# A decode-attention kernel: the first weight load issued ahead of the program's entry barrier

## The chip, the cores and the metric

The kernel runs on one core of one Trainium2 chip. The metric is the time of one execution in microseconds (us), as the device counts it; every time quoted is the median of several executions. The profile's span (first to last instruction) is 1.7 to 2.0 us shorter than that time, in every run. The ranges are quoted with the medians.

The engines are called TensorE (PE in the profile), VectorE (DVE), ScalarE (ACT), GpSimd (POOL) and SyncE (SP).

## The reference

One token passes through a layer norm; attention over a key and a value cache of 8 groups with 65,536 keys each runs beside a small dense block with GELU; both results are added to x.

```python
x = A_x                                       # 1 x 1 x 512, bf16
xn = layernorm(x)
q = xn @ wq                                   # 512 x 4096
s = q . k_cache * 128 ** -0.5                 # k_cache: 8 x 65536 x 128, four heads to a group
o = softmax(s) . v_cache                      # v_cache: 8 x 65536 x 128
out = x + o @ wo + (gelu(xn @ w1 + b1) @ w2 + b2)
```

The two caches are 134 MB each, wq and wo 4 MB each, w1 and w2 1.8 MB each: 280 MB have to be read once, and very little else is large.

## The kernel before

All bulk loads are issued by SyncE on one DMA queue, in the order in which they are used: wq, w1, w2, then K and V pieces of 4 or 8 MB as their buffers come free, then wo. The three small inputs (x, b2, b1) are issued by ScalarE on its own queue.

```python
def dma_small():                              # ScalarE's queue
    sch.dma(ACT, lambda: act.dma_start(out=rows_bf[0:1, :], in_=A_x[0]), sem_x, writes=["row0"])
    ...                                       # b2 and b1 likewise

def dma_wq():                                 # SyncE's queue
    sch.dma(SP, lambda: sp.dma_start(out=wq_sb, in_=A_wq.rearrange("(p kt) n -> p kt n", kt=KT)),
            csem[NK], writes=["va"])
...
dma_small()
dma_wq()
dma_w12()
issue_chunks()                                # K0 and K1; V0 only when the dense block has left its buffer
```

Operations are first recorded per engine (`SP.ops` and so on, each with its waits and the semaphore that it raises) and written out at the end, one block per engine. Ahead of these blocks stands what the framework puts at the head of every program: GpSimd writes four constants, then all five engines meet at a barrier. Each engine drains itself and raises one semaphore; GpSimd waits for four of these and releases the others. (In the trace of the kernel before, the four drains start between 0.00 and 0.32 us, GpSimd's last constant is finished at 0.45, its wait for the four starts at 0.54, and the others are released at 0.66 to 0.68.) No load needs the constants.

Then come the layer norm (VectorE, from x), the q projection (TensorE, from wq), the dense block (w1, w2), and 16 rounds over pairs of K pieces and a V piece. `va` and `vb` are the two halves of the V buffer. They hold wq, w1 and w2 first, so the first V load is issued only when the dense block is through.

Of the kernel before, what the change touches and what calls it, by code (L numbers as in the profile page):

```python
# [183 lines left out]
def _emit(eng_obj, ops):  # L184
    for waits, fn, pub in ops:
        for s, v in waits:
            eng_obj.wait_ge(s, v)
        if fn is None:
            continue
        ins = fn()  # L190
        if pub is not None:
            ins.then_inc(pub[0], pub[1])


def _emit_rolled(eng_obj, ops, marks, holder=None):
    folded, growth = _fold([ops[a:b] for a, b in zip(marks, marks[1:])])
    _emit(eng_obj, ops[:marks[0]])
    _emit_loop(eng_obj, folded, growth, len(marks) - 1, holder)
    _emit(eng_obj, ops[marks[-1]:])
# [38 lines left out]
def bass_parallel_sum__gqa_block_cached__dense_activation_gelu__decode_kernel(  # L238
# [48 lines left out]
    SP = sch.add_engine("sp", "sp")  # L287
# [49 lines left out]
    while g0 < GE:  # L337
        n = next(m for m in (4, 2, 1) if g0 + m <= GE)
# [487 lines left out]
    )  # L826
    sch.wait_ev(SP, ev_out)

    with nc.Block() as block:

        @block.gpsimd
        def _(e):
            _emit(e, POOL.ops)

        @block.sync
        def _(e):
            _emit(e, SP.ops)

        @block.scalar
        def _(e):  # L840
            _emit_rolled(e, ACT.ops, [m[1] for m in marks2])

        @block.vector
        def _(e):
            _emit_rolled(e, DVE.ops, [m[0] for m in marks2], pair)

        @block.tensor
        def _(e):
            _emit_rolled(e, PE.ops, marks)
# [28 lines left out]
```

## Time and profile before

| | before |
|---|---|
| time | 658.46 us (658.15 to 658.76, 3 runs) |
| span, TensorE busy, granted TensorE clock | 656.5 us, 82%, 0.767 |
| read from HBM | 280.50 MB, 427 GB/s over the span |
| wq issued, first wq packet, barrier open | 0.75, 1.79, 0.66 us |
| last weight piece landed | 653.7 us |

Lines of the page, kernel before: the span, the DMA engines' busy share in tenths and the rate in each of 40 slices, and the chain of work that ended last by engine.

```profile
span 656.5 us, 27968 instructions
...
DMA  8999999999999999999999999999999999999997
GB/s 369 438 436 426 429 430 433 439 425 461 401 441 439 421 453 413 437 427 445 433 417 449 417 445 421 427 457 411 447 419 447 429 419 441 423 459 408 431 433 295
...
DMA 63%; PE 34%; issue 2%; DVE 0%; SPq 0%
...
```

The DMA engines are busy at 90% or more in all slices but the first and the last, and 63% of the last chain is waiting for DMA. Between the 50th and the 200th MB the packets' records show (200 - 50) MB / (466.32 - 120.13) us = 433 GB/s. Whether the stream could run faster is not shown here; the change leaves its rate as it is and goes for time in which the stream doesn't run, before its first packet at 1.79 us.

The timeline of the kernel before, from 0 us; the columns are start, duration, engine (SPq and ACTq are the sequencers that issue loads), line, operation and tiles.

```profile
...
0.33 0.12 POOL L863 MEMSET const-uint8-127<- 128x1 uint8 x1
0.74 0.53 ACTq L454 DMA_DIRECT2D rows_bf<-in_A_x_dram  x1
...
0.75 0.39 SPq L463 DMA_DIRECT2D kv<-in_A_wq_dram  x1
...
1.20 0.41 SPq L467 DMA_DIRECT2D kv<-in_B_w_dram  x1
...
2.95 0.40 DVE L499 CAST x_row<-rows_bf 1x512 f32<-1x512 bf16 x1
...
8.75 0.16 DVE L521 CAST xnT_bf<-pA 128x4 bf16<-128x4 f32 x1 [0.38 <-PE pA L518]
...
13.13 3.53 PE L525 MATMUL pss<-kv,xnT_bf 128*1 128x512 bf16 x32 [4.42 <-DMA kv<-in_A_wq_dram]
...
```

GpSimd's last constant is finished at 0.45 us, the barrier opens, and SyncE issues wq at 0.75 us. x has landed before VectorE takes it up at 2.95 us; the layer norm's end (L521) is at 8.91 us; and TensorE's q projection (L525) waits, by the bracket, for wq, until 13.13 us.

The waits of SyncE's queue in the kernel before (waited for: us in total, times, longest):

```profile
...
SPq L434 <- PE pst L590: 350.8, 30, 17.1
...
SPq L863 <- PEq L863: 0.7, 1, 0.7
...
```

The second line is the entry barrier: SyncE stands there for 0.7 us. The first is the opposite: SyncE waits 30 times for TensorE to free a K buffer, 351 us in total, and this costs nothing, as enough loads are in the queue meanwhile. That can be counted. With the bytes of all loads issued, less the bytes of all packets finished, at each issue of SyncE, the least that was outstanding in the kernel before is 2.33 MB (at 113.90 us), which is 5.4 us of work at 433 GB/s. The queue is never empty between its first and its last packet. The packets' records agree: from 2.5 us to 640 us at least 13 packets are in flight at every moment, and nearly always 16 or more.

The end of the last chain in the kernel before, in order of time (start, duration, what):

```profile
...
585.82 28.78 DMA kv<-in_A_k_cache_dram
...
636.99 16.42 DMA kv<-in_A_wo_dram
653.41 0.14 issue
653.55 0.63 PE pss L805 x13
...
654.20 0.29 DVE fin_bf L820
```

### The profile page before, as it was taken

The page shows a single profiled execution, that of the slowest core. Times are in us where ns is not written, and L with a number is a line of the kernel's source. Part 1 is how long each engine was busy: PE and PEld are TensorE (multiplying, and loading weights), DVE is VectorE, ACT ScalarE, POOL GpSimd, SP SyncE. Part 2 cuts the span into 40 slices and gives each one's busy share as a digit, 9 for nine tenths or more (in the row PEclk, how much of TensorE's full clock was granted, in tenths as well). Part 3 has the DMA queues.
Part 4 walks back from the last instruction along what each step waited for, and adds up shares of the span by engine and source line. Part 5 has one row for each costly group of instructions (what it writes and reads, how often), then busy time and mean ns, then how long its engine had stood idle before and what let it go on. Part 6 is the DMA issues. An engine that isn't in the chain of part 4 may idle for free.

```text
span 656.5 us, 27968 instructions
## 1 busy us (share of the span) xinstructions
PE 539.3 (82%) x12682; PEld 512.1 (78%) x12682; DVE 275.7 (42%) x574; ACT 244.9 (37%) x454; POOL 2.9 (0%) x27
## 2 busy tenths in 40 slices
PE   2388699999789797878969787896978879797897
PEld 0187698988689697868969786896968779686896
DVE  3244162635435172442616245171634516254353
ACT  0134153534425152351605335161443516144251
POOL 0000000000000000000000000000000000000000
PEclk9788597878759596885959778596877859687595
DMA  8999999999999999999999999999999999999997
GB/s 369 438 436 426 429 430 433 439 425 461 401 441 439 421 453 413 437 427 445 433 417 449 417 445 421 427 457 411 447 419 447 429 419 441 423 459 408 431 433 295
DMA packets 8774, 280.65 MB, mean 427 GB/s; under 512 B 1082, under 2 KB 1596, under 8 KB 1724
## 3 DMA queue, kind: packets, MB, share of 16 engines
q1 hardware_dynamic: 8616, 280.50, 99.2%
q8 instruction: 8, 0.13, 0.1%
q10 hardware_dynamic: 148, 0.01, 0.0%
q14 instruction: 2, 0.02, 0.0%
HBM read 280.50 MB, written 0.00 MB: 427 GB/s over the span
## 4 chain that ended last, share of the span: by engine, by line
DMA 63%; PE 34%; issue 2%; DVE 0%; SPq 0%
DMA kv<-in_A_k_cache_dram 61%; PE pst L590 27%; PE pss L610 4%; DMA kv<-in_A_wo_dram 3%; PE pO L681 2%; PE pA L637 0%; PE pA L648 0%; DVE pmax L618 0%; PE pA L697 0%; PE pss L805 0%; DVE gmax L639 0%; DVE diag L641 0%; SPq L470 0%; SPq L467 0%; SPq L463 0%
## 5 line engine op out<-in xcount | busy, mean ns | idle before, releaser
L590 PE MATMUL pst<-ident_bf,kv 128*128 128x128 bf16 x4096 | 284.3, 236 | 34.0 <-DMA kv<-in_A_k_cache_dram 33.9
L600 ACT ACTIVATE kt_ring<-pst 128x1024 bf16<-128x1024 bf16 x192 | 195.6, 1027 | 312.1 <-PE pst L590 310.7
L590 PEld LDWEIGHTS pst<-ident_bf,kv 128*128 128x128 bf16 x4096 | 266.0, 107 | 42.4 <-DMA kv<-in_A_k_cache_dram 35.5
L598 DVE COPY kt_ring<-pst 128x1024 bf16<-128x1024 bf16 x320 | 210.7, 687 | 121.1 <-PE pst L590 118.7
L681 PE MATMUL pO<-P_bf,kv 128*128 128x4 bf16 x4096 | 115.1, 166 | 37.1 <-DMA kv<-in_A_v_cache_dram 32.1
L681 PEld LDWEIGHTS pO<-P_bf,kv 128*128 128x128 bf16 x4096 | 113.6, 104 | 38.5 <-DMA kv<-in_A_v_cache_dram 33.1
L610 PE MATMUL pss<-q_cur,kt_ring 128*128 128x4 bf16 x4096 | 111.9, 164 | 4.9 <-issue 4.9
L610 PEld LDWEIGHTS pss<-q_cur,kt_ring 128*128 128x128 bf16 x4096 | 109.3, 96 | 5.1 <-issue 5.1
L659 ACT ACTIVATE P_bf<-pss,negm 128x128 bf16<-128x128 f32 x128 | 50.9, 547 | 67.6 <-DVE negm L651 67.6
L690 DVE COPY o_all<-pO 128x4 f32 (+1 forms) x32 | 5.2, 161 | 120.3 <-PE pO L681 119.5
L618 DVE TENSOR_REDUCE pmax<-pss 128x4 f32<-128x512 f32 x32 | 22.1, 691 | 68.8 <-PE pss L610 68.8
L659 ACT ACTIVATION_READ_ACCUMULATOR P_bf<-pss,negm 128x1 f32 x128 | 35.3, 276 | 0.0
L648 PEld LDWEIGHTS pA<-diag,ones_f 4*128 4x128 f32 x64 | 12.6, 245 | 17.8 <-DVE diag L641 16.2
L637 PE MATMUL pA<-ident_f,pmax 128*4 128x128 f32 x64 | 14.0, 305 | 12.5 <-DVE pmax L618 12.5
L648 PE MATMUL pA<-diag,ones_f 4*128 4x4 f32 x64 | 15.4, 309 | 10.0 <-DVE diag L641 10.0
L637 PEld LDWEIGHTS pA<-ident_f,pmax 128*4 128x4 f32 x64 | 2.9, 84 | 15.7 <-DVE pmax L618 14.0
L639 DVE TENSOR_REDUCE gmax<-pA 4x1 f32<-4x128 f32 x32 | 8.8, 274 | 9.1 <-PE pA L637 9.1
L673 DVE COPY sums_all<-sums 128x8 f32 (+1 forms) x16 | 2.7, 171 | 23.4 <-ACT P_bf L659 23.4
L697 PE MATMUL pA<-sums_all,ones_f 128*128 128x128 f32 x32 | 12.4, 491 | 0.0
L651 DVE TENSOR_SCALAR negm<-pA 128x4 f32<-128x4 f32 x32 | 5.1, 161 | 10.8 <-PE pA L648 10.8
L697 PEld LDWEIGHTS pA<-sums_all,ones_f 128*128 128x128 f32 x32 | 8.1, 312 | 0.0
L641 DVE TENSOR_SCALAR diag<-ident_f,gmax 4x4 f32<-4x4 f32 x32 | 7.0, 218 | 1.1
(78 smaller groups left out, 49.5 us busy)
## 6 DMA issues: line engine op xcount, KB each, us to landing
kv<-in_A_k_cache_dram SPq DMA_DIRECT2D x32, 4096.0 KB, 27.5
kv<-in_A_v_cache_dram SPq DMA_DIRECT2D x4, 4096.0 KB, 23.2
kv<-in_A_wq_dram SPq DMA_DIRECT2D x1, 4096.0 KB, 12.2
kv<-in_B_w_dram SPq DMA_DIRECT2D x2, 1792.0 KB, 18.0
kv<-in_A_wo_dram SPq DMA_DIRECT2D x1, 2048.0 KB, 23.0
kv<-in_A_wo_dram SPq DMA_DIRECT2D x1, 1024.0 KB, 25.1
kv<-in_A_wo_dram SPq DMA_DIRECT2D x1, 512.0 KB, 25.9
kv<-in_A_wo_dram SPq DMA_DIRECT2D x1, 384.0 KB, 16.4
```

The costliest lines, as they stand in the source:

```text
L590: lambda tb=tb, at=at, b=b, tt=s * TPB + t: pe.transpose(pst[tb][:, at * 128:(at + 1) * 128], slot[b][:, tt, :], ident_bf[:, :]),
L598: e, fn = DVE, lambda tb=tb, dst=dst: dve.tensor_copy(out=dst, in_=pst[tb][:, :])
L600: e, fn = ACT, lambda tb=tb, dst=dst: act.activation(out=dst, in_=pst[tb][:, :], func=ACTF.Copy)
L610: lambda k=k, kb=kb, at=at, t=t: pe.matmul(pss[k][:, at:at + HPG], lhsT=kt_ring[:, kb * BCOL + t * 128:kb * BCOL + (t + 1) * 128], rhs=q_c ...
L618: lambda k=k: dve.tensor_reduce(out=pmax[:, :], in_=pss[k][:, 0:CW].rearrange("p (t j) -> p j t", j=HPG), axis=AX.X, op=ALU.max),
L637: sch.op(PE, lambda: pe.matmul(pA[0:HPG, PA_ST:PA_ST + 128], lhsT=pmax[:, 0:HPG], rhs=ident_f[:, :], start=True, stop=True), reads=["pmax" ...
L639: sch.op(DVE, lambda: dve.tensor_reduce(out=gmax4[:, :], in_=pA[0:HPG, PA_ST:PA_ST + 128], axis=AX.X, op=ALU.max), reads=["pA"], writes=[" ...
L641: sch.op(DVE, lambda: dve.tensor_scalar(out=diag4[:, :], in0=ident_f[0:HPG, 0:HPG], scalar1=gmax4[0:HPG, 0:1], scalar2=None, op0=ALU.mult) ...
L648: sch.op(PE, lambda: pe.matmul(pA[:, PA_SB:PA_SB + HPG], lhsT=ones_f[0:HPG, 0:128], rhs=diag4[0:HPG, 0:HPG], start=True, stop=True), reads ...
L659: lambda k=k, at=at, j=j, src=src: act.activation(out=P_v[k][:, :, j], in_=src[:, :, j], func=ACTF.Exp, bias=negm[:, at:at + 1], scale=1.0 ...
L681: lambda k=k, t=t: pe.matmul(pO[:, 0:HPG], lhsT=vslot[:, k * TPD + t, :], rhs=P_v[k][:, t, :], start=t == 0, stop=t == TPD - 1),
L697: sch.op(PE, lambda: pe.matmul(pA[:, PA_SUM:PA_SUM + NC], lhsT=ones_f[:, :], rhs=sums_all[:, :], start=True, stop=True), reads=["ones_f", ...
```

## The change

The intent is to take the barrier's wait off the stream's start. The record of the first load is taken from SyncE's list and its instruction is put into the head of the program, ahead of the drain with which SyncE reports to the barrier. That is legal because the load depends on nothing, and the other engines still learn by its semaphore that it has landed (12.34 us in the changed kernel, 13.00 before; the record marks the result of every experiment as correct).

```diff
     sch.wait_ev(SP, ev_out)
 
+    first = SP.ops.pop(0)
+    assert not first[0]
+    head = nc.cur_bb.bb.instructions
+    n = len(head)
+    first[1]().then_inc(*first[2])
+    at = next(k for k, ins in enumerate(head) if ins.engine == mybir.EngineType.SP
+              and type(ins).__name__ == "InstDrain")
+    moved = [head.pop() for _ in range(len(head) - n)]
+    for ins in moved:
+        head.insert(at, ins)
+
     with nc.Block() as block:
```

## The prediction

> **What bounds the kernel.** Bytes. The page shows 280.5 MB read from HBM at 427 GB/s over a span of 656.5 us, DMA busy share 0.9 or more in 38 of 40 slices. The chain of waits is 63% DMA, 61% of the span the K-cache loads. Setting each issue of SyncE (timeline) against the packets finished by then, the queue never runs dry: from the first packet at 1.79 us to the last weight at about 653.4 us, at least 2.3 MB are outstanding at every issue (the least at 113.9 us, usually 4 to 8 MB).
>
> **What the change moves.** No work is added or removed. In the timeline SyncE reaches the entry barrier first: its drain is the instruction that begins the span, at 0.00. GpSimd's four constant memsets end at 0.45 us, its drain at 0.50, the barrier opens at 0.66 us (the waits view: SyncE waits 0.7 us there once), and the wq load is issued at 0.75 us; its first packet starts at 1.79 us, 1.04 us later. In the changed program the load stands before SyncE's drain, so it should issue at 0.00 to 0.05 us. Issuing takes 0.39 us; the drain then arrives at about 0.45 us, before GpSimd checks at 0.54 us, so the barrier should still open at about 0.66 us. The later loads issue 0.45 us earlier, but queue behind wq, so this is worth nothing of its own.
>
> **How much is on the path.** As the queue is never empty, all of the stream should move with its first packet: 0.70 to 0.75 us earlier. The last wo piece lands at 653.7 us and should land near 653.0; the 2.8 us after it are unchanged. TensorE's tail is almost as late: its wo matmuls end about 0.5 us before the last piece lands. But that tail starts from the K load landing at 614.6 us, which moves as well, so I expect nearly all to come through, unless the granted clock (0.5 from 645 us on) falls differently.
>
> **What it costs.** x is asked for by ScalarE at 0.74 us and lands at 2.02, just ahead of wq's packets. It will now be behind them. [...] b2's packet, issued by 1.52 us among wq's 32 KB packets, starts at 6.07. I estimate that x lands at 5 to 6 us, the layernorm chain (2.95 to 8.91 us, 6 us long) ends at 11 to 12, and wq is in by about 12.4. At worst the q projection starts 1 us later than that; the first V load hangs on it, issued at 25.3 us with 6.8 MB (about 16 us) outstanding, so this slack swallows it.
>
> **Prediction.** 658.46 - 0.73 = 657.7 us; 8 in 10: 657.2 to 658.3. Faster by over 2%: 0.3%; within 2%: 99.3%; slower by over 2%: 0.4%.
>
> **What shows it.** wq issue at about 0 and its first packet near 1.05 us; barrier still open near 0.66; x landing and layernorm later by some 3 us; every K load landing 0.7 us earlier, also at the end; span 655.8 us.
>
> **What would make it wrong.** The barrier opens late because the drain waits for more than the issue. The chip's time does not start with the span. x so late that the V0 issue comes after the queue is empty. HBM rate varying between runs by 0.1% (0.65 us), which would hide the gain. A different clock phase in the tail.

(The 5 to 6 us for x are an estimate from the one packet of b2 that the trace of the kernel before shows.)

## The result

| | before | after |
|---|---|---|
| time | 658.44 us (658.15 to 658.76, 6 runs) | 657.64 us (657.41 to 657.74, 6 runs) |
| span | 656.5 us | 655.7 us |
| wq issued | 0.75 us | 0.00 us |
| first wq packet | 1.79 us | 1.02 us |
| barrier open | 0.66 us | 0.71 us |
| x landed | 2.02 us | 6.97 us |
| last weight piece landed | 653.73 us | 653.03 us |
| granted TensorE clock | 0.767 | 0.770 |

The ratio is 0.9988, with a 95% interval of 0.9975 to 1.0001. (A ratio is the mean time of one kernel's runs over that of the other's of the same rounds, so it is not quite the ratio of the medians.) By the interval the gain of 0.80 us is just not told from nothing; but no run of the changed kernel is as slow as the fastest of before, here or in the repetition below.

The page of the changed kernel, the same lines:

```profile
span 655.7 us, 27968 instructions
...
DMA  9999999999999999999999999999999999999997
GB/s 387 444 447 410 429 432 434 444 420 448 420 444 428 420 460 404 448 418 456 430 418 442 426 454 410 434 448 416 448 420 444 430 418 448 416 464 402 438 426 303
...
DMA 64%; PE 34%; issue 2%; DVE 0%; SPq 0%
...
```

The first slice now moves 387 GB/s in place of 369, and the rest is the same to within what slices scatter. The timeline:

```profile
...
0.00 0.39 SPq L463 DMA_DIRECT2D kv<-in_A_wq_dram  x1
...
0.33 0.12 POOL L874 MEMSET const-uint8-127<- 128x1 uint8 x1
0.79 0.52 ACTq L454 DMA_DIRECT2D rows_bf<-in_A_x_dram  x1
...
0.80 0.33 SPq L467 DMA_DIRECT2D kv<-in_B_w_dram  x1
...
7.07 0.41 DVE L499 CAST x_row<-rows_bf 1x512 f32<-1x512 bf16 x1 [3.98 <-DMA rows_bf<-in_A_x_dram]
...
12.89 0.16 DVE L521 CAST xnT_bf<-pA 128x4 bf16<-128x4 f32 x1 [0.39 <-PE pA L518]
...
13.11 3.51 PE L525 MATMUL pss<-kv,xnT_bf 128*1 128x512 bf16 x32 [0.25 <-DVE xnT_bf L521]
...
```

wq leads from 0.00 us. x is now taken up at 7.07 us, its bracket (not shown before, as there was no wait) naming the load of x, and the q projection waits for the layer norm's result (xnT_bf) in place of wq. It starts at 13.11 us, where it started before. The waits of SyncE's queue:

```profile
...
SPq L434 <- PE pst L590: 348.8, 30, 16.8
...
SPq L874 <- PEq L874: 0.2, 1, 0.2
...
```

The barrier's wait has shrunk from 0.7 to 0.2 us (the line is another, as the file is longer). The end of the last chain:

```profile
...
585.42 28.49 DMA kv<-in_A_k_cache_dram
...
634.98 17.73 DMA kv<-in_A_wo_dram
652.71 0.14 issue
652.85 0.49 PE pss L805 x16
...
653.36 0.29 DVE fin_bf L820
```

The K load of the last round ends at 585.42 + 28.49 = 613.91 us; before, at 585.82 + 28.78 = 614.60. So the stream is 0.69 us ahead after 614 us of it, as it was at its start. The piece that TensorE waits for at the very end lands at 653.03 us (634.98 + 17.73, and 0.32 for the last small piece behind it), 0.70 us earlier than before.

Where is the shift made, and is any of it lost? The next table is worked out from the packets' records: for each kernel the time at which so many MB of the stream had landed, less the same time in the kernel before. It includes the experiments, and the text comes back to it. The first column of times is before's own.

```
   MB   before   after  rest_late  wq_late  wq_later  x_after_w1  x_after_k0   split  split_cols
    2     7.70   -0.71      -0.68     1.67      7.08       -0.88       -0.74    4.13       -0.82
    6    16.84   -0.71      -0.67     1.63      7.03       -0.93       -0.79    8.03       -0.82
   16    40.29   -0.67      -0.52     1.72      7.14       -0.81       -0.74    8.08       -0.74
   17    42.89   -0.70      -0.68     1.61      7.03        0.71       15.88    8.06       -0.86
   50   120.13   -0.64      -0.56     1.70      7.04        1.35       16.51    8.15       -0.74
  200   466.32   -0.68      -0.70     1.54      6.91        0.69       16.39    8.33       -0.76
280.4   652.50   -0.73      -0.64     1.70      7.02        0.64       16.46    7.98       -0.70
```

Column "after": the shift is there in the first 2 MB, and it is the same to 0.1 us down to the last packet. The profile's end has 0.14 us more than the stream gave: from the last piece's landing to the issue of the output it took 654.52 - 653.73 = 0.79 us before and 653.68 - 653.03 = 0.65 us after, where the last matmuls took 0.49 us in place of 0.63. This is the granted TensorE clock, which in these traces changes between 1.0 and 0.5: in the 0.5 us after the last landing it was 0.50 before and 1.00 after. In the profiled execution of the repetition below it was 0.50 again, this stretch took 0.78 us, the span was 0.60 us shorter than before's, and the last piece had landed 0.61 us earlier. (Likewise the last matmuls took 0.48 and 0.49 us in wq_late and x_act_early, at full clock, and 0.62 in rest_late and five_early, at half.) So the clock can be worth 0.14 us in one execution; it is not the gain.

### The profile page after: what moved, and what is told of

The parts are those of the page before. It is cut to its first block, busy times and chain, and to the rows that moved or that the text cites. A ratio compares the mean times of both kernels' runs of the same rounds, so it can differ in the third digit from the quotient of the medians. Undisturbed runs are those within 1.5% of the kernel's fastest.

```text
span 655.7 us, 27968 instructions
## 1 busy us (share of the span) xinstructions
PE 536.8 (82%) x12682; PEld 509.0 (78%) x12682; DVE 275.7 (42%) x574; ACT 245.2 (37%) x454; POOL 2.9 (0%) x27
## 4 chain that ended last, share of the span: by engine, by line
DMA 64%; PE 34%; issue 2%; DVE 0%; SPq 0%
DMA kv<-in_A_k_cache_dram 61%; PE pst L590 27%; PE pss L610 4%; DMA kv<-in_A_wo_dram 3%; PE pO L681 2%; PE pA L637 0%; PE pA L648 0%; DVE pmax L618 0%; PE pA L697 0%; DVE gmax L639 0%; PE pss L805 0%; DVE diag L641 0%; SPq L470 0%; SPq L467 0%; DVE fin_bf L820 0%
## 5 line engine op out<-in xcount | busy, mean ns | idle before, releaser
L590 PE MATMUL pst<-ident_bf,kv 128*128 128x128 bf16 x4096 | 281.4, 235 | 34.3 <-DMA kv<-in_A_k_cache_dram 34.2
L590 PEld LDWEIGHTS pst<-ident_bf,kv 128*128 128x128 bf16 x4096 | 263.2, 106 | 42.5 <-DMA kv<-in_A_k_cache_dram 35.7
```

The source lines that it names most:

```text
L590: lambda tb=tb, at=at, b=b, tt=s * TPB + t: pe.transpose(pst[tb][:, at * 128:(at + 1) * 128], slot[b][:, tt, :], ident_bf[:, :]),
```

## The experiments

The theories:

- **A.** The stream of loads is one queue that is never empty. The time moves with its first packet, by as much, and with nothing else at the start.
- **B.** The gain came from the later loads (w1, w2, K0, K1), which are also issued 0.4 to 0.6 us earlier.
- **C.** The first microsecond isn't on the path; the gain came from the clock phase of TensorE's tail (whether the last matmuls fall into a stretch of full or of half granted clock).
- **D.** It is chance.
- **The side effect.** x lands 5 us later. Either the slack behind it swallows this, or it eats part of a larger gain.

All kernels of one group ran on the same chip, with the kernel before among them. There are four groups, on four chips: the first four runs, the next four, the next three, and split_cols alone. All outputs are right.

| run | time, us (range, runs) | before beside it, us | ratio to before (95%) |
|---|---|---|---|
| after_again | 657.71 (657.33 to 657.84, 5) | 658.44 | 0.9988 (0.9974 to 1.0001) |
| wq_late | 660.02 (659.91 to 660.08, 5) | 658.44 | 1.0025 (1.0011 to 1.0039) |
| rest_late | 657.72 (657.62 to 657.81, 5) | 658.44 | 0.9989 (0.9976 to 1.0003) |
| five_early | 657.65 (657.54 to 657.72, 5) | 658.44 | 0.9988 (0.9974 to 1.0002) |
| wq_later | 665.47 (665.24 to 665.59, 4) | 658.31 | 1.0109 (1.0094 to 1.0125) |
| x_after_wq | 657.66 (657.58 to 658.54, 5) | 658.31 | 0.9990 (0.9976 to 1.0003) |
| x_after_k0 | 674.04 (673.50 to 675.77, 4) | 658.31 | 1.0236 (1.0220 to 1.0252) |
| x_act_early | 657.50 (657.41 to 657.71, 5) | 658.31 | 0.9988 (0.9974 to 1.0002) |
| x_after_wq_again | 657.58 (657.44 to 658.07, 5) | 658.37 | 0.9988 (0.9975 to 1.0001) |
| x_after_w1 | 659.49 (659.00 to 662.24, 6) | 658.37 | 1.0029 (1.0015 to 1.0042) |
| split | 666.48 (666.44 to 666.61, 4) | 658.37 | 1.0124 (1.0109 to 1.0138) |
| split_cols | 657.61 (657.35 to 657.73, 5) | 658.37 | 0.9986 (0.9973 to 1.0000) |

### The changed kernel again

No edit.

> The changed kernel once more, beside the others, as their yardstick. Theory A (the whole stream of loads is one never empty queue, so the time moves with the first packet of wq and with nothing else): 0.7 to 0.8 us under before, about 657.65 us, first packet at 1.02 us, last wo piece landing at 653.0 us. Theory D (the gain of the first measurement is a chance of the rounds): the gap closes to under 0.3 us.

Measured: 657.71 us beside 658.44, again 0.73 us and the same ratio. The eleven runs of the changed kernel lie between 657.33 and 657.84 us; no run of the kernel before, in any of the groups, is under 658.06. D falls, though each interval alone reaches 1.

### wq later instead of earlier, two doses

The kernel before, with SyncE held at wq until GpSimd has written its last constant; in the second run with 20 more constant writes ahead of that one.

```diff
-                csem[NK], writes=["va"])
+                csem[NK], reads=["ones2"], writes=["va"])
```
```diff
     sch.op(POOL, lambda: pool.memset(ones_f[:, :], 1.0), writes=["ones_f"])
+    for _ in range(20):
+        sch.op(POOL, lambda: pool.memset(ones_f[:, :], 1.0), writes=["ones_f"])
     sch.op(POOL, lambda: pool.memset(ones2_bf[:, :], 1.0), writes=["ones2"])
```

> The kernel before, with SyncE waiting for GpSimd's last constant (written at 2.37 us) ahead of the wq load. wq and all later loads are issued some 1.6 to 1.7 us later than before. Theory A: slope 1, so 660.1 us (1.65 us over before) and 2.4 us over the changed kernel. Theory C (the first microsecond is not on the path: the queue has slack somewhere, and the gain came from the clock phase in TensorE's tail): under 0.5 us over before.

> As wq_late, with 20 more constant writes of GpSimd ahead (about 0.19 us each), so that wq is issued 5 to 6 us later than before, about 6.1 us. A second dose for the slope. Theory A: slope 1 of the first packet's shift, so about 663.8 us (5.4 us over before). Theory C: under 1 us over before. A slope under 1 would show that the stream catches part of a delay up.

SyncE's issues of wq in the timelines of wq_late and of wq_later (the line differs as the file does):

```profile
...
2.39 0.39 SPq L463 DMA_DIRECT2D kv<-in_A_wq_dram  x1
...
```
```profile
...
7.82 0.39 SPq L465 DMA_DIRECT2D kv<-in_A_wq_dram  x1
...
```

The second dose came out larger than I had expected: with the 20 further constant writes wq was issued 7.07 us later than in the kernel before (7.82 against 0.75 us), not 5.4, so the expected time was missed while the slope was not. With the first packet's time:

| kernel | first packet, us | against before | time against before beside it | slope |
|---|---|---|---|---|
| after | 1.02 | -0.78 | -0.80 | 1.03 |
| wq_late | 3.41 | +1.62 | +1.58 | 0.98 |
| wq_later | 8.83 | +7.03 | +7.16 | 1.02 |

(Differences are taken before rounding.) One microsecond at the first packet was one microsecond at the end, in both directions and up to nine times the size of the change. C falls: the clock phase was worth 0.14 us above, and could not follow such doses. The columns wq_late and wq_later of the stream's table show, within 0.25 us, that the delay is neither caught up nor grows on the way.

### wq early, everything behind it late

The changed kernel, with w1 and all loads after it held until GpSimd's last constant.

```diff
-            in_=B_w1.rearrange("(p kt) f -> p kt f", kt=KT)), sem_w1, writes=["w1"])
+            in_=B_w1.rearrange("(p kt) f -> p kt f", kt=KT)), sem_w1, reads=["ones2"], writes=["w1"])
```

> The changed kernel, wq still ahead of the barrier, but w1 and all loads after it held until GpSimd's last constant, issued at about 2.4 us in place of 0.80 us, later than even in before (1.20 us). Theory A: as the changed kernel, 657.65 us within 0.2, as these loads wait in the queue behind wq's 4.2 MB until about 11 us anyway. Theory B (the gain came from w1, w2 and the K loads being issued 0.4 to 0.5 us earlier): 658.4 us or more, the gain gone.

SyncE's issues in the timeline of rest_late:

```profile
...
0.00 0.39 SPq L463 DMA_DIRECT2D kv<-in_A_wq_dram  x1
2.44 0.33 SPq L467 DMA_DIRECT2D kv<-in_B_w_dram  x1
...
```

w1 is issued at 2.44 us, 1.24 us later than even before the change, and the time is 657.72 us: the gain stands whole. B falls. wq's 4.2 MB keep the DMA engines busy until about 12 us (in the changed kernel wq's last packet ends at 11.97 us), so what stands behind wq could come 1.24 us later than before at no cost; still later was not tried.

### All five first loads ahead of the barrier

```diff
-    first = SP.ops.pop(0)
-    assert not first[0]
+    firsts = [SP.ops.pop(0) for _ in range(5)]
+    assert not any(f[0] for f in firsts)
```
(and each is then written out in place of the one)

> All five first loads of SyncE ahead of the barrier. SyncE then arrives at the barrier at about 2.3 us, so the other engines start about 1.7 us later, x is asked for at about 2.5 us. Theory A: as the changed kernel, 657.65 us within 0.2, though x lands some microseconds later still (8 to 10 us in place of 6.97) and the q projection starts at 14 to 16 us in place of 13.1. Theory B (earlier issue of the later loads pays): up to 0.5 us faster. If late x or late engines count: slower by 1 to 2 us.

Measured: 657.65 us. The barrier opens only at 2.75 us, x lands at 8.33 us, the q projection starts at 14.46 us, and none of this costs anything. Earlier issue of the later loads gives nothing either, which is the other side of rest_late.

### x early, and x later still

In x_act_early ScalarE's load of x is moved ahead of the barrier too, in the same way as wq. In the other three ScalarE waits for a bulk load before it asks for x: wq, w1 or the first K piece.

```diff
-        sch.dma(ACT, lambda: act.dma_start(out=rows_bf[0:1, :], in_=A_x[0]), sem_x, writes=["row0"])
+        sch.dma(ACT, lambda: act.dma_start(out=rows_bf[0:1, :], in_=A_x[0]), sem_x, reads=["va"], writes=["row0"])
```
(`reads=["w1"]` and `reads=["slot0"]` in the other two, with the call of `dma_small()` moved behind that of the load)

> The changed kernel with ScalarE's load of x ahead of the barrier too. x is asked for at about 0.1 us and should land by about 1.5 to 2.5 us if its packet comes ahead of wq's, or at about 5 us if it comes just behind; the barrier opens at about 0.9 us. The q projection can then start as wq lands, at about 12.4 us in place of 13.1. Theory A: no gain, 657.65 us within 0.2. Rival (x being late costs part of the gain): 0.3 to 0.7 us faster than the changed kernel.

> The changed kernel, with x asked for only after wq has landed, at about 12 us in place of 0.79, so it lands at about 16 us in place of 6.97 and the q projection starts at about 22 us in place of 13.1, the first V load is issued at about 34 us in place of 25.3, with some 2.5 MB outstanding. Theory A with my reading that the slack swallows x's delay: 657.65 us within 0.3. Rival (the later x already eats some of the gain): 1 us or more slower than the changed kernel.

> The changed kernel, with x asked for only after the first K load has landed, at about 30 us. x lands at about 35 us, the q projection starts at about 41 us, the first V load is issued at about 54 us, when the queue has been empty since about 39.7 us. Theory A says that this is where the slack ends: the stream stands still for 14 to 16 us, and the time is 671 to 674 us, its end moved by just the empty time. If the time stays under 660 us, the queue is not what counts.

> The changed kernel, with x asked for after w1 has landed, at about 16.9 us: x lands at about 21.5 us and the first V load is issued at about 39.7 us, just as the queue runs empty (39.7 us). Between x_after_wq (no loss in the median) and x_after_k0 (16 us lost), this should be the edge: the queue stands empty for the 1 us from issue to first packet, 658.0 to 659.5 us.

> x_after_wq once more, for a second trace: the profiled run of the first was its slowest (658.54 us, the other four 657.58 to 657.68 us). Theory A: median 657.65 us within 0.2 again; if the profiled run is one of the common ones, its byte stream should run 0.7 us ahead of before from end to end, with about 2 MB outstanding at the first V issue.

The timeline of x_act_early:

```profile
...
0.12 0.52 ACTq L454 DMA_DIRECT2D rows_bf<-in_A_x_dram  x1
...
9.06 0.16 DVE L521 CAST xnT_bf<-pA 128x4 bf16<-128x4 f32 x1 [0.38 <-PE pA L518]
...
12.48 1.88 PE L525 MATMUL pss<-kv,xnT_bf 128*1 128x512 bf16 x16 [3.45 <-DMA kv<-in_A_wq_dram]
...
```

x lands at 1.35 us, the layer norm ends at 9.22 us, and the q projection starts as soon as wq is in, at 12.48 us in place of 13.11. The time, 657.50 us, is 0.14 to 0.21 us under the changed kernel's two medians, on another chip and with overlapping ranges. Against the kernel before beside it the gain is 0.81 us, as in the changed kernel (0.80): no part of a gain was hidden behind x.

The other direction shows how much slack there is:

| kernel | x landed, us | first V load issued, us | outstanding then, MB | time, us |
|---|---|---|---|---|
| x_act_early | 1.35 | 23.83 | 7.08 | 657.50 |
| after | 6.97 | 25.27 | 6.36 | 657.64 |
| x_after_wq_again | 17.64 | 35.14 | 2.13 | 657.58 |
| x_after_w1 | 20.94 | 39.25 | 0.49 | 659.49 |
| x_after_k0 | 36.37 | 54.51 | 0 | 674.04 |

With x landed up to 10.7 us later than in the changed kernel nothing is lost in the median. At x_after_w1 the edge is reached: the V load is issued with 0.49 MB left, 1.1 us of work, and it takes about 1 us from the issue to the first packet (1.01 to 1.04 us for wq in these traces); no packet was in flight for 0.35 us, and the stream's table steps from -0.81 to +0.71 us at just that place. (The profile is of the fastest of its six executions; two others took 660.95 and 662.24 us, which no trace explains. Its 1.35 us at 50 MB is no further loss: the loads issued after the first V load land 0.62 to 0.70 us later than before, to the end.) At x_after_k0 the queue stood empty for 15.2 us, and the step is -0.74 to 15.88 us. (This profile is of the slowest of four executions, 675.77 us; it lost more later, as told below. Both medians came out at or just over the top of what I had expected: the step of 16.62 us here is 1.4 us more than the empty time.) The windows view of x_after_k0 (stretch, its length, busy time of the engines, then clock, DMA share and GB/s), over the gap and after it:

```profile
...
40.00:55.50 15.50, 10.40 (x107) 4.97 (x108) 4.49 (x15) 3.23 (x5) 0.00 (x0) 0.89 0.07 22
...
100.00:600.00 500.00, 428.50 (x10178) 412.34 (x10177) 215.15 (x436) 198.65 (x367) 1.17 (x13) 0.77 1.00 432
...
```

22 GB/s in the gap, and 432 GB/s afterwards: the time lost isn't made up. This is the same as at the start, at another place: what counted is whether the queue was empty.

How thin may the margin be? In both runs of x_after_wq the profiled execution was the slowest (658.54 and 658.07 us); the other eight lie between 657.44 and 657.72 us. In the first, the landings show where the time went. Up to the K load landing near 120 us its stream runs 0.84 us ahead of before. The next V load, issued at 115.53 us with only 1.31 MB outstanding, lands 0.04 us behind before, and every later load stays there, within 0.1 us; the last K piece lands at 614.66 us, where the changed kernel has 613.91. Between 117.13 and 119.01 us only 15 packets were in flight. (Every trace has some seven such stretches of about 1.0 us among its first loads, at no cost; this one is longer, and no other trace has it.) So 0.88 us were lost at one load, with 3 us of work still outstanding in total; the execution took 0.91 us more than the median of the other four. In x_after_k0's profile the same V load was issued with 1.21 MB outstanding, and there the landings' delay against before grew from 15.79 to 17.22 us; in x_after_w1's it was issued with 1.02 MB and lost nothing. In the kernel before, 2.33 MB were enough. Why the 0.88 us were lost is not shown; nor was it settled what made the second run's execution slow.

### A smaller first load

By theory A only the first packet counts, and it comes 1.02 us after the issue. The question of `split` was whether a small load's first packet comes sooner.

```diff
-        sch.dma(SP, lambda: sp.dma_start(out=wq_sb, in_=A_wq.rearrange("(p kt) n -> p kt n", kt=KT)),
-                csem[NK], writes=["va"])
+        src = A_wq.rearrange("(p kt) n -> p kt n", kt=KT)
+        for rows in (slice(0, 16), slice(16, 128)):
+            sch.dma(SP, lambda rows=rows: sp.dma_start(out=wq_sb[rows], in_=src[rows]),
+                    csem[NK], writes=["va"], total=32)
```

> The changed kernel with wq in two loads: 16 rows[...] ahead of the barrier, 112 rows right after it. The question is what the 1.02 us from issue to first packet consist of. If the issue must be written out whole before packets start (0.39 us for 128 rows), the small load's first packet starts at 0.7 to 0.8 us and by theory A the time falls by as much, to about 657.4 us; if the 1.02 us are a latency whatever the size, the first packet stays at 1.0 us and the time at 657.65 us.

Measured: the first packet starts at 1.03 us, so the small load's packet comes no sooner. But the issue of 16 rows took as long as that of 128 (0.40 and 0.39 us), so the run can't tell a latency from the issue's start from a wait for the issue's end. Traces show, for the first packet of wq, 1.01 to 1.04 us from the issue's start, and 0.61 to 0.66 us from its end.

But neither answer had the time: 666.48 us, 8.8 us slower than the changed kernel. The queue never ran empty here (at least 3.51 MB outstanding at each issue after the first loads), so theory A needs a condition that it didn't state: that the packets keep their rate. The windows view of split over the first load:

```profile
...
2.00:12.00 10.00, 0.03 (x1) 0.04 (x2) 4.56 (x12) 1.49 (x2) 0.43 (x3) 1.00 0.86 203
12.00:20.00 8.00, 0.26 (x4) 0.17 (x4) 0.16 (x1) 0.00 (x0) 0.00 (x0) 1.00 0.91 225
...
```

and of the changed kernel:

```profile
...
2.00:12.00 10.00, 0.00 (x0) 0.00 (x0) 4.05 (x12) 1.49 (x2) 0.42 (x3) 1.00 0.92 395
12.00:20.00 8.00, 6.22 (x72) 2.39 (x72) 1.96 (x5) 1.88 (x2) 0.00 (x0) 1.00 1.02 437
...
```

The DMA engines are as busy as ever (0.86 and 0.91) but move half: 203 and 225 GB/s in place of 395 and 437. A 32 KB packet takes 2.16 us in the median, in place of 1.21. The 112 rows are slow by themselves: the 96 packets that started after 6.9 us, when the first 16 rows had landed, took 2.10 us. The last run asks whether it is the rows or the fact of two loads:

```diff
+        for part in (slice(0, 1), slice(1, KT)):
+            sch.dma(SP, lambda part=part: sp.dma_start(out=wq_sb[:, part, :], in_=src[:, part, :]),
+                    csem[NK], writes=["va"], total=32)
```

> wq in two loads again, but cut by columns: 128 rows of 8 KB ahead of the barrier, 128 rows of 24 KB after it. split (16 rows, then 112) was 8.8 us slower than the changed kernel, as wq's 32 KB packets took 1.8 to 3.6 us each in place of 1.21. Theory E (the rows chosen are the cause[...]): cut by columns the packets keep their rate (some 27 GB/s for each engine), wq is in by about 12 us, and the time is 657.65 us within 0.3. Rival F (two loads in place of one, whatever the rows, are the cause): 660 us or more, wq in after 15 us.

(E is judged by the packets' rate and the time alone. The 27 GB/s are an estimate: 32 KB in the 1.21 us that wq's packets take in the changed kernel.)

Measured: 657.61 us, as the changed kernel, with wq's last packet finished at 11.84 us (11.97 in the changed kernel, 20.72 in split). The windows view of split_cols:

```profile
...
2.00:12.00 10.00, 0.29 (x4) 0.21 (x4) 4.72 (x13) 1.49 (x2) 0.41 (x3) 1.00 1.01 426
12.00:20.00 8.00, 6.30 (x71) 2.48 (x71) 1.61 (x3) 1.88 (x2) 0.00 (x0) 1.00 1.05 449
...
```

So two loads are harmless, and the choice of rows costs the 8.8 us; F falls. In split the first 16 rows' 0.52 MB took 4.3 us from the first packet's start to the last one's end, 123 GB/s, and 5.8 us to the landing, 90 GB/s. No run here shows why the rows cost so much; it stays open.

No experiment beat the changed kernel by more than the scatter: the variants with wq issued at 0.00 us and no harm done lie at 657.50 to 657.72 us.

## Why the prediction was right

- **What bounds the kernel.** Right. Delays of the first packet by -0.78, +1.62 and +7.03 us changed the time by -0.80, +1.58 and +7.16 us.
- **The size.** 0.73 us predicted, 0.80 and 0.73 us measured in two groups; 657.7 us against 657.64. The shift at the stream's end is 0.70 us.
- **The barrier.** "The barrier should still open at about 0.66 us" was off by 0.05 us. SyncE's drain took 115 ns behind the load and 7 ns bare, and GpSimd's wait ended after it. The records of the sequencers' instructions (start us, duration ns), which the views leave out:

```
before  SyncE drain  0.000    7     GpSimd's wait for all four  0.543     released  0.664
after   SyncE drain  0.452  115     GpSimd's wait for all four  0.593     released  0.713
```

  It cost nothing, as five_early shows with a barrier at 2.75 us.
- **The cost of x.** That x would land behind wq's packets was right, and the size too small: x lands at 6.97 us, not at 5 to 6, and the layer norm ends at 13.05 us, not at 11 to 12. The packets' records name the term that was missed. x's data packet did end within the forecast, at 5.44 us, but the 4-byte packet that follows it on ScalarE's queue started only at 6.65 us, 1.21 us later, as long as one of wq's packets takes (1.21 us in the median); in the kernel before it started at 1.72 us, as the data packet ended. In both kernels x's semaphore rose 0.3 us after that packet's end (1.73 and 2.02 us before, 6.66 and 6.97 us after). So the small load waited twice here, and took 6.18 us from issue to landing in place of 1.28. The q projection therefore starts when it did before (13.1 us) and not with wq's earlier arrival. That the slack swallows it was right, and x_after_wq_again shows that in the median it would swallow 10.7 us more.
- **Later loads are worth nothing of their own.** Right, by rest_late (657.72 us) and five_early (657.65 us).
- **The tail.** Right that it moves with the K load that starts it (613.91 us in place of 614.60).

## What to carry to other kernels

In this kernel, whose transfer queue never runs empty, three things counted: when its first packet started (shifts of -0.78 to +7.03 us came out as -0.80 to +7.16 us of time), the rate that its packets kept (203 to 225 GB/s in place of 395 to 437 over split's first load: 8.8 us), and what followed the last (0.14 us). So ask first, at each issue, how many bytes are still outstanding. The margin had to be more than nothing: with 2.33 MB no time was lost here, with 1.0 to 1.3 MB time was lost in two of three profiles. The first load of such a stream is worth trying ahead of everything that it doesn't depend on, the framework's own barrier included: it gave 0.73 and 0.80 us here. Small loads that are asked for at the same time may then land behind it, as x did here (6.97 us in place of 2.02), which has to be checked against their slack. If a load has to be cut, try the cut by columns first, so that each part keeps all 128 partitions: it cost nothing here, and the one cut by rows that was tried (16 and 112) cost 8.8 us.
